# Attention with a gating MLP on one core: where the MLP's seven products are summed, when its matmuls are due, and which engine makes the normalisation's small operations

## The chip, the cores and the metric

One core of one Trainium2 chip. The metric is the time of one execution on the device in microseconds (us), lower is better. The kernel before takes 3404.55 us, the median of three runs (3404.28 to 3408.29).

## What is computed

```python
def _A_ref(x, wqkv, wo):                      # H = 32 heads of 32
    q, k, v = ...                             # x @ wqkv, split by head
    scores = einsum("bhqd,bhkd->bhqk", q, k) * Dh ** -0.5
    p = softmax(scores, axis=-1)
    o = einsum("bhqk,bhkd->bhqd", p, v)
    return o.reshape(B, S, D) @ wo
def _B_ref(x, w1, b1, w2):                    # F = 3584
    h = einsum("bsd,df->bsf", x, w1) + b1
    return einsum("bsf,fd->bsd", mish(h), w2)
xn = layernorm(x)
out = x + _A_ref(xn, wqkv, wo) * silu(_B_ref(xn, w1, b1, w2))
```

Here x is 2048 x 1024, wqkv 1024 x 3072, wo 1024 x 1024, w1 1024 x 3584 and w2 3584 x 1024, all in 32-bit floats.

## The kernel before

Every 32-bit operand of the large matmuls is split into a high part (a copy in the type fp32r, `copy`, ACT, L276) and the rest (`low`, a subtraction, DVE or GpSimd, L284), and each product is made as three matmuls, `THREE`: high x high, high x rest, rest x high. The 2048 rows are 16 tiles of 128 (`NT`), or four chunks of 512 (`NC`). The normalised and transposed x of chunk c stands in `xc0` to `xc3`.

**Stage 1, normalisation and the first pass of v** (to about 85 us). Tile after tile: `x_load` (an issue on SP, the SyncE queue), `ln_a` (statistics on DVE, L398 to L400), `ln_r` (ln and exp on ACT, for the inverse root), `ln_b` (four DVE operations on 128 x 1: one Newton step on the root `rs`, and the shift `tmp`), `ln_x` (the scaling on ACT, L273), `ln_t` (eight transposes on PE, L426), `ln_c` (the split of the transposed tile into `xc`, ACT and DVE). One loop with index t from 2 to 17 runs these for neighbouring tiles, and in between `v_group` (PE, L325) multiplies the tiles that are there with the first 256 columns of v. Instructions of an engine run in the order in which this loop writes them. Beside it, GpSimd splits the first `W1_0` tiles of w1 (`w1_first`): loaded into the two buffers `first_w1`, split into halves of `xc2` and `xc3` that no x tile has reached yet, and moved from there to the DRAM scratch `w1s` (512 KB read and as much written). Each tile of w1 passes through steps 0 (load), 1 (split) and 2 (move) in the iterations n + 2, n + 3 and n + 5:

```python
for step, n in enumerate((t - 2, t - 3, t - 5)):
    if 0 <= n < W1_0:
        w1_first(n, step)
```

Later tiles of w1, up to number 21, are split by GpSimd in the following passes over v.

**Stage 2, q and k** (to about 552 us): the projections `qk`, with splits of w1 and w2 on GpSimd beside them.

**Stage 3, attention and MLP** (to about 3220 us). A planner (`Plan`) merges five streams of operations into one order for each engine. Every operation has an estimated duration, needs, buffers that it takes and gives, and a key, its due time; a simulated clock picks what comes next by these. Attention: scores twice, once for the maximum (`s`, PE; `mx`, DVE) and once transposed (`t`, PE; exponential `p`, ACT); `z`, the sums of the exponentials over tiles, 128 x 2048 additions on GpSimd (L919, 4.6 us each); `pv` (PE). The MLP runs between: `h` (PE), mish (ACT and DVE, some on GpSimd), and `y`. For two of the 28 tiles of F at a time (a pair, `U` = 14 in each chunk) a Strassen scheme makes seven products of 256 x 512, which DVE adds onto seven accumulators, `yacc` (L1213). The due time of a y matmul is set by two numbers, in units of the time of an h tile (g runs from 0 to about 8 within a pair):

```python
g = (2 * j + s + (i + 1) / 3) * 4 / 7
due = 2 * B + 2 + Y0 + g * Y1 + (BEHIND if B >= NC * U - 2 else 0)
```

At the end of each chunk `y_sums` adds the seven products up to the four blocks of y: seven GpSimd additions of 128 x 1024 (L1226), with four stores to the scratch `ys` (SP), each after the sums that it needs. The accumulators are free for the next chunk when those that read them are through.

**Stage 4, the tail** (to the end). The output projection (`op`, L1317) of chunk 0 runs at the end of the plan (`p_stream`), as do the splits of wo. Behind the plan, for chunks 1 to 3: the attention's output is loaded (`oraw`, SP), split (`split_o`: ACT, then DVE, into `ohl` or `xo`), and multiplied tile by tile. For each tile `start` loads x (`x3`) and the finished y (`y3`), ACT makes the silu, and `end` multiplies and adds on DVE (L1420, L1421) and stores to out (issued on ACT's queue, L1425). `x3` and `y3` have six buffers each.

## Time and profile before

| | |
|---|---|
| median of three runs | 3404.55 us |
| the profiled execution | 3404.78 us |
| its span in the trace | 3403.0 us |
| PE (matmul) busy | 3350.0 us, 98% |
| PE weight loads | 2444.7 us, 72% |
| DVE (VectorE) | 2683.6 us, 79% |
| ACT (ScalarE) | 2039.2 us, 60% |
| POOL (GpSimd) | 2727.3 us, 80% |
| read from and written to HBM | 474.97 MB and 160.69 MB |

The span runs from the first instruction to the last; the 1.8 us between it and the execution's time lie around the program. Busy shares are means over four stages with different limits, so what a change in one stage is worth has to be read from that stage. Weight loads run beside matmuls. The profile names tiles without their numbers, and L stands for a line of the listing above.

### The profile page before, as it was taken

The numbers are of one execution on the slowest core, as the hardware profiler recorded it, in microseconds if no ns is written. First come the engines' busy times: TensorE is split into PE (matmuls) and PEld (weight loads), VectorE is DVE, ScalarE is ACT, GpSimd is POOL, SyncE is SP. The second block draws the span as 40 slices with busy tenths as digits, with TensorE's granted clock in tenths as the row PEclk, the third lists the DMA queues.
The fourth block names the chain that finished last, engine by engine and source line by source line (L and its number), as shares of the span: only waits on it lengthen the run. The fifth ranks groups of instructions, "written<-read, shape, count | busy, mean of one in ns | idle before, by whom it ended". The sixth has DMA issues, their size and how long they took to land.

```text
span 3403.0 us, 48050 instructions
## 1 busy us (share of the span) xinstructions
PE 3350.0 (98%) x17107; PEld 2444.7 (72%) x17107; DVE 2683.6 (79%) x4462; ACT 2039.2 (60%) x3394; POOL 2727.3 (80%) x923
## 2 busy tenths in 40 slices
PE   8999999999999999999999999999999999999999
PEld 8898887767766766667777676666776666677587
DVE  6024446999999998889999988889999889896753
ACT  6112222766766667767776677667776776677621
POOL 3547662998898989999989899989988999899910
PEclk9999999999999999999999999999999999999999
DMA  8989997544555465545455564445556555546582
GB/s 285 339 307 370 369 367 243 143 137 138 154 150 148 144 192 180 149 131 153 141 157 157 182 186 137 140 141 148 149 164 198 163 149 158 150 146 193 171 306 85
DMA packets 257633, 639.87 MB, mean 188 GB/s; under 512 B 90266, under 2 KB 99482, under 8 KB 248730
## 3 DMA queue, kind: packets, MB, share of 16 engines
q1 hardware_dynamic: 254948, 628.42, 58.7%
q10 hardware_dynamic: 2448, 8.39, 0.6%
q8 instruction: 136, 2.23, 0.3%
q14 instruction: 101, 0.83, 0.1%
HBM read 474.97 MB, written 160.69 MB: 187 GB/s over the span
## 4 chain that ended last, share of the span: by engine, by line
PE 84%; DVE 7%; DMA 3%; POOL 2%; issue 2%; ACT 1%; SPq 1%; ACTq 0%; DVEq 0%; POOLq 0%
PE h L1049 16%; PE y L1190 13%; PE pv L938 13%; PE s L803 12%; PE t L890 12%; PE qk L725 8%; PE op L1317 4%; PE v L325 4%; DVE mx L809 2%; DMA kstack<-ks 1%; POOL z L919 1%; DVE yacc L1213 1%; ACT p L273 1%; PE zp L974 1%; POOL pw L284 1%
## 5 line engine op out<-in xcount | busy, mean ns | idle before, releaser
L919 POOL TENSOR_TENSOR z<-z,p 128x2048 f32<-128x2048 f32 x448 | 2066.5, 4613 | 75.0 <-ACT p L273 50.6
L273 ACT ACTIVATE p<-t,zero 128x512 f32<-128x512 f32 x2048 | 1366.5, 689 | 455.8 <-PE t L890 436.0
L809 DVE TENSOR_REDUCE mx<-s 128x1 f32<-128x512 f32 x1984 | 1283.4, 682 | 65.9 <-PE s L803 63.4
L890 PE MATMUL t<-qstack,kstack 128*128 128x512 f32 x2048 | 791.3, 394 | 1.8 <-ACT p L273 0.9
L803 PE MATMUL s<-kstack,qstack 128*128 128x512 f32 x1984 | 755.6, 397 | 14.8 <-DMA kstack<-ks 7.5
L1049 PE MATMUL h<-xr,w 128*128 128x512 f32 x2016 | 676.6, 390 | 1.4 <-DVE aw L284 0.6
L1213 DVE TENSOR_TENSOR yacc<-yacc,y 128x512 f32<-128x512 f32 x728 | 492.6, 680 | 36.8 <-PE y L1190 33.3
L803 PEld LDWEIGHTS s<-kstack,qstack 128*128 128x128 f32 x1984 | 366.8, 188 | 160.8 <-issue 26.8
L890 PEld LDWEIGHTS t<-qstack,kstack 128*128 128x128 f32 x2048 | 382.0, 188 | 126.5 <-issue 28.5
L938 PE MATMUL pv<-p,v 128*32 128x512 f32 x4096 | 466.0, 595 | 1.0 <-ACT p L273 0.6
L1049 PEld LDWEIGHTS h<-xr,w 128*128 128x128 f32 x2016 | 377.6, 188 | 84.1 <-DVE aw L284 2.1
L725 PE MATMUL qk<-xc,qkw 128*128 128x512 f32 x1536 | 351.3, 389 | 0.3
L725 PEld LDWEIGHTS qk<-xc,qkw 128*128 128x128 f32 x1536 | 288.0, 188 | 60.8 <-DVE mx L607 1.2
L938 PEld LDWEIGHTS pv<-p,v 128*32 128x32 f32 x4096 | 119.9, 109 | 276.4 <-issue 247.6
L919 POOL TENSOR_TENSOR z<-p,p 128x2048 f32<-128x2048 f32 x32 | 147.8, 4620 | 159.5 <-PE zp L974 107.1
L1190 PE MATMUL y<-w,az 128*128 128x512 f32 x672 | 232.1, 395 | 4.7 <-POOL az L284 1.7
L1190 PE MATMUL y<-w,ay 128*128 128x512 f32 x672 | 227.2, 391 | 3.4 <-ACT ay L276 1.4
L1190 PE MATMUL y<-w,ax 128*128 128x512 f32 x672 | 225.1, 391 | 2.2 <-DVE ax L284 0.7
L1049 PE MATMUL h<-xc,w 128*128 128x512 f32 x672 | 225.7, 391 | 0.0
L950 DVE TENSOR_TENSOR o<-o,pv 128x512 f32<-128x512 f32 x96 | 65.9, 687 | 117.0 <-PE pv L938 112.9
L1190 PEld LDWEIGHTS y<-w,az 128*128 128x128 f32 x672 | 125.1, 189 | 37.1 <-DVE yacc L1213 3.1
L1190 PEld LDWEIGHTS y<-w,ay 128*128 128x128 f32 x672 | 125.2, 188 | 33.2 <-DVE yacc L1213 3.5
(134 smaller groups left out, 3627.8 us busy)
## 6 DMA issues: line engine op xcount, KB each, us to landing
w<-w2s SPq DMA_DIRECT2D x392, 512.0 KB
w<-w1s SPq DMA_DIRECT2D x224, 512.0 KB
w2s<-pw SPq DMA_DIRECT2D x98, 512.0 KB
qstack<-qs SPq DMA_DIRECT2D x96, 256.0 KB
kstack<-ks SPq DMA_DIRECT2D x96, 256.0 KB
w1s<-w1h SPq DMA_DIRECT2D x34, 512.0 KB
x<-in_A_x_dram SPq DMA_DIRECT2D x32, 512.0 KB
qs<-qst SPq DMA_DIRECT2D x32, 512.0 KB
```

The costliest lines, as they stand in the source:

```text
L273: nc.scalar.activation(out_, in_, fn, bias=zero if bias is None else bias, scale=scale)
L325: nc.tensor.matmul(ps[:, :cols], xc[t // 4][:, a, k, (t % 4) * P:(t % 4 + 1) * P], w(b, k), start=n == 0, stop=n == 3 * KT - 1)
L725: nc.tensor.matmul(ps, w[:, k // 4, a, k % 4], xc[c][:, b, k], start=n == 0, stop=n == 3 * KT - 1)
L803: nc.tensor.matmul(sp_, qst[h % 3][:, qt * P:(qt + 1) * P], kst[h % 3][:, kc * 512:(kc + 1) * 512], start=True, stop=True)
L809: nc.vector.reduce_max(tiles["mx"][:, qt, kc:kc + 1], tiles[qt, kc], axis=AX.X)
L890: nc.tensor.matmul(tp, kst[h % 3][:, kt * P:(kt + 1) * P], qst[h % 3][:, c * 512:(c + 1) * 512], start=True, stop=True)
L919: nc.gpsimd.tensor_tensor(zs[h], pts[T - 1] if kt == 1 else zs[h], pts[T], ALU.add)
L938: nc.tensor.matmul(t["b"][c * DH:(c + 1) * DH, :], vt[h][:, k, :], pts[T - kt + k][:, c * 512:(c + 1) * 512], start=k == kt - size + 1, st ...
L1049: nc.tensor.matmul(t["h"], w1t[m_][:, a, k % 4], xts_[c][:, b, k], start=i == 0, stop=i == 3 * KT - 1)
L1190: nc.tensor.matmul(t["y"], acts[B, kind][:, p, half * 256 + s * P:half * 256 + (s + 1) * P], w2t[m_][:, q], start=i == 0, stop=i == 2)
L1213: nc.vector.tensor_tensor(ya, ya, t["y"], ALU.subtract)
L1317: nc.tensor.matmul(ps[t, dh], ohl[t // 4, k][:, a, s * P:(s + 1) * P], wt[k][b][:, r], start=k == 0 and i == 0, stop=k == KT - 1 and i == 2)
```

## The change

Five edits. (1) `W1_0` is 3 instead of 4; all three tiles of w1 are staged in `xc3`, each half is split in an iteration of its own (t = 5 to 10), and the moves stand in iterations 7, 9 and 11 (before: 5 to 8). The first x tile is loaded and scaled in two halves. (2) From the third tile on, `ln_b` runs on GpSimd, as six operations with two inputs or one. (3) `Y1` is 0.18 instead of 0.14. (4) For chunks 1 to 3 `y_store` stores the seven products as they are, each after DVE's last addition to it; `ys` holds seven blocks of 256 x 512 for each chunk, 3.67 MB instead of 2.1. Chunk 0 keeps `y_sums`. (5) In the tail the blocks are loaded into `yp` in two calls, one at the first tile of the chunk before and one at its second; at its third tile `y_total` adds them up on GpSimd, and the silu is made in two halves. `x3` has five buffers.

```diff
@@ -24,7 +24,7 @@
-W1_0, W1_V = 4, 21
+W1_0, W1_V = 3, 21
 
 PACE = 1.95
 NS = H * NT
@@ -36,7 +36,7 @@
 
-PS, ACTS, W1S, W2S, Y0, Y1 = 6, 4, 3, 3, 1.2, 0.14
+PS, ACTS, W1S, W2S, Y0, Y1 = 6, 4, 3, 3, 1.2, 0.18
 
@@ -243,7 +243,7 @@
-    ys = [dram.tile([P, 4, D], F32, name=f"ys{i}") for i in range(NC)]
+    ys = [dram.tile([P, 7, 2, 512], F32, name=f"ys{i}") for i in range(NC)]
@@ -359,27 +359,27 @@
 
     def x_load(t):
         xt = vp.tile([P, D], F32, tag="x", name=f"x{t}", bufs=5)
-        nc.sync.dma_start(xt, x[t * P:(t + 1) * P, :])
+        for r in (slice(0, 512), slice(512, D)) if t == 0 else (slice(0, D),):
+            nc.sync.dma_start(xt[:, r], x[t * P:(t + 1) * P, r])
         return xt
 
     first_w1 = [p.tile([P, 2, KT, P], F32, tag=tag, name=f"w1f{tag}") for p, tag in ((w1p, "z0"), (big, "w"))]
 
-    def split_w(w, raw, job=False):
-        for half in range(2):
+    def split_w(w, raw, job=False, halves=range(2)):
+        for half in halves:
             r = slice(half * 4, half * 4 + 4)
             p = w[half] if isinstance(w, list) else w[:, half]
             (nc.gpsimd if job else nc.vector).tensor_copy(p[:, 0], raw[:, r])
             low(nc.gpsimd if job else nc.vector, p[:, 1], raw[:, r], p[:, 0])
 
     def w1_first(n, step):
-        t, g = xc[2 + n // 2], n % 2
-        raw = first_w1[n // 2][:, g]
-        w = t[:, 1, 4 * g:4 * g + 4].rearrange("p k n -> p (k n)") \
+        raw = first_w1[n // 2][:, n % 2]
+        w = xc[NC - 1][:, n // 2, 4 * (n % 2):4 * (n % 2) + 4].rearrange("p k n -> p (k n)") \
             .rearrange("p (h a k f) -> p h a k f", h=2, a=2, f=P)
         if step == 0:
             nc.sync.dma_start(raw, w1[n])
-        elif step == 1:
-            split_w(w, raw, True)
+        elif step < 3:
+            split_w(w, raw, True, (step - 1,))
         else:
             move(w1s[n], w)
 
@@ -408,6 +408,16 @@
     def ln_b(t):
         mv, var, rs = stat.pop(t)
         tmps[t] = tmp = vp.tile([P, 1], F32, tag="tmp", name=f"tmp{t}", bufs=3)
+        if t > 1:
+            g = nc.gpsimd
+            g.tensor_tensor(tmp, rs, var, ALU.mult)
+            g.tensor_tensor(tmp, tmp, rs, ALU.mult)
+            g.tensor_scalar(tmp, tmp, -0.5, 1.5, op0=ALU.mult, op1=ALU.add)
+            g.tensor_tensor(rs, rs, tmp, ALU.mult)
+            g.tensor_tensor(tmp, mv[:, 0:1], rs, ALU.mult)
+            g.tensor_scalar(tmp, tmp, -1.0, 0.0, op0=ALU.mult, op1=ALU.add)
+            tmps[t] = tmp, rs
+            return
         nc.vector.scalar_tensor_tensor(tmp, rs, var, rs, op0=ALU.mult, op1=ALU.mult)
         nc.vector.tensor_scalar(tmp, tmp, -0.5, 1.5, op0=ALU.mult, op1=ALU.add)
         nc.vector.tensor_tensor(rs, rs, tmp, ALU.mult)
@@ -416,7 +426,8 @@
 
     def ln_x(t):
         tmp, rs = tmps.pop(t)
-        act(xts[t], xts[t], AF.Identity, bias=tmp, scale=rs)
+        for r in (slice(0, 512), slice(512, D)) if t == 0 else (slice(0, D),):
+            act(xts[t][:, r], xts[t][:, r], AF.Identity, bias=tmp, scale=rs)
 
     def ln_t(t):
         xt = xts.pop(t)
@@ -475,8 +486,11 @@
         if t + 1 < NT:
             ln_r(t + 1)
         evac()
-        for step, n in enumerate((t - 2, t - 3, t - 5)):
-            if 0 <= n < W1_0:
+        if t - 2 < W1_0:
+            w1_first(t - 2, 0)
+        for step in (3, 1, 2):
+            n, odd = divmod(t - 4 - step, 2)
+            if not odd and 0 <= n < W1_0:
                 w1_first(n, step)
         if t == NT - 3:
             vraw = {(i, 0): v_load(1 + i, 0) for i in range(2)}
@@ -1214,7 +1228,7 @@
                     done[j, s] = op("DVE" if b else "ACT", 0.69 if b else 0.6, emit=y_add, urgent=U_Y,
                                     give=[("d", t["own"]), ("b", t["own"])], need=[m] + ([free[j]] if j in free and b == 0 else []))
             if b == U - 1:
-                free = y_sums(c, done)
+                free = (y_store if c else y_sums)(c, done)
         final["y"] = m
 
     def y_sums(c, done):
@@ -1227,23 +1241,30 @@
             last[i] = free[i] = free[j] = o
             return o
 
-        def store(j, rh, dh):
+        def store(j):
             def emit(at):
-                nc.sync.dma_start(ys[c][:, 2 * rh:2 * rh + 2, dh * 512:(dh + 1) * 512], yacc[:, j])
+                nc.sync.dma_start(ys[c][:, j], yacc[:, j])
             free[j] = op("SP", 0.1, need=[last[j]], emit=emit, bytes_=P * 1024 * 4)
 
         add_(4, 0)
         add_(0, 2)
-        store(0, 0, 0)
+        store(0)
         add_(1, 4)
         add_(3, 1)
-        store(3, 1, 0)
+        store(3)
         add_(4, 5)
         add_(4, 6)
-        store(4, 0, 1)
+        store(4)
         add_(5, 1)
-        store(5, 1, 1)
+        store(5)
         return free
+
+    def y_store(c, done):
+        def store(j):
+            return op("SP", 0.1, need=[done[j, i] for i in range(2)], bytes_=P * 1024 * 4,
+                      emit=lambda at: nc.sync.dma_start(ys[c][:, j], yacc[:, j]))
+
+        return {j: store(j) for j in range(7)}
 
@@ -1389,7 +1410,8 @@
     ph = ExitStack()
     op_ = pool(ph, "op", 8)
     rp = pool(ph, "rp", 8, side="right")
-    xp = pool(ph, "xp", 6, side="right")
+    xp = pool(ph, "xp", 5, side="right")
+    yp = pool(ph, "yp", 2, side="right")
     oraw = {}
 
     def new_o(c, k):
@@ -1408,17 +1430,33 @@
         low(nc.vector, o[:, 1], raw, o[:, 0])
 
     xt, yt = {}, {}
+    BLOCK = {(0, 0): 0, (1, 0): 3, (0, 1): 4, (1, 1): 5}
 
     def start(t):
         xt[t] = xp.tile([P, D], F32, tag="x3", name=f"x3_{t}")
         nc.sync.dma_start(xt[t], x[t * P:(t + 1) * P, :])
-        yt[t] = xp.tile([P, D], F32, tag="y3", name=f"y3_{t}")
-        nc.sync.dma_start(yt[t], ys[t // 4][:, t % 4])
+
+    def y_load(c, js):
+        for j in js:
+            yt[c, j] = yp.tile([P, 2, 512], F32, tag=f"y{j}", name=f"yp{c}_{j}", bufs=2 if j in BLOCK.values() else 1)
+            nc.sync.dma_start(yt[c, j], ys[c][:, j])
+
+    def y_total(c):
+        for i, j in ((4, 0), (0, 2), (1, 4), (4, 5), (4, 6), (3, 1), (5, 1)):
+            nc.gpsimd.tensor_tensor(yt[c, i], yt[c, i], yt[c, j], ALU.add)
+
+    def silu(t):
+        c, s = divmod(t, 4)
+        for dh in range(2):
+            y = yt[c, BLOCK[s // 2, dh]][:, s % 2]
+            act(y, y, AF.Silu)
 
     def end(t, dh):
+        c, s = divmod(t, 4)
+        y = yt[c, BLOCK[s // 2, dh]][:, s % 2]
         r = slice(dh * 512, dh * 512 + 512)
-        nc.vector.tensor_tensor(yt[t][:, r], ps[t, dh], yt[t][:, r], ALU.mult)
-        nc.vector.tensor_tensor(xt[t][:, r], xt[t][:, r], yt[t][:, r], ALU.add)
+        nc.vector.tensor_tensor(y, ps[t, dh], y, ALU.mult)
+        nc.vector.tensor_tensor(xt[t][:, r], xt[t][:, r], y, ALU.add)
         if t == NT - 1:
             nc.scalar.dma_start(out[t * P:, r], xt[t][:, r])
         elif dh:
@@ -1426,9 +1464,13 @@
 
     for k in range(KT):
         new_o(1, k)
-    for t in range(4):
-        start(t)
-    act(yt[0], yt[0], AF.Silu)
+    start(0)
+    y_load(0, (0, 4))
+    start(1)
+    y_load(0, (3, 5))
+    start(2)
+    start(3)
+    silu(0)
     for k in range(4):
         split_o(1, k)
     for c in range(NC):
@@ -1436,12 +1478,16 @@
             t = 4 * c + s
             if t + 4 < NT:
                 start(t + 4)
+            if c + 1 < NC and s < 2:
+                y_load(c + 1, ((4, 0, 2, 1), (5, 6, 3))[s])
+            if c + 1 < NC and s == 2:
+                y_total(c + 1)
             for dh in range(2):
                 k = 2 * s + dh
                 if c + 1 < NC and (c or k > 3):
                     split_o(c + 1, k)
                 if dh == 0 and t + 1 < NT:
-                    act(yt[t + 1], yt[t + 1], AF.Silu)
+                    silu(t + 1)
                 if c:
                     n = 2 * s + dh
                     ps[t, dh] = bank({"b": bank_of[n]}, f"op{t}_{dh}")
```

What this does to the engines' order is shown at three places, by the lines of each kernel's own listing (the changed kernel's are 14 higher in the plan and 23 to 38 higher in the tail).

**The normalisation, around tile 6.** First DVE's instructions before the change: `st`, `mv` and `var` are the statistics of tile 7, `rs6` and `tmp6` root and shift of tile 6, and the last two rows are the split of tile 5's transposes (`pt5`).

```order
L398 BN_STATS st7_504<-x7_372 128x6 x2
L399 BN_AGGR mv7_505<-st7_504 128x2
L400 TENSOR_SCALAR var7_506<-mv7_505 128x1
L411 SCALAR_TENSOR_TENSOR tmp6_523<-rs6_442,var6_441 128x1
L412 TENSOR_SCALAR tmp6_523<-tmp6_523 128x1
L413 TENSOR_TENSOR rs6_442<-rs6_442,tmp6_523 128x1
L414 SCALAR_TENSOR_TENSOR tmp6_523<-mv6_440,rs6_442 128x1
L284 TENSOR_TENSOR xc1_173<-pt5_0_537,xc1_173 128x4x128
L284 TENSOR_TENSOR xc1_173<-pt5_1_542,xc1_173 128x4x128
```

GpSimd's instructions there after the change; `w1fz0` is a loaded tile of w1, and the rows on `xc3` are the two operations of a half of its split.

```order
L372 CAST xc3_175<-w1fz0_179 128x512
L284 TENSOR_TENSOR xc3_175<-w1fz0_179,xc3_175 128x512
L413 TENSOR_TENSOR tmp6_521<-rs6_446,var6_445 128x1
L414 TENSOR_TENSOR tmp6_521<-tmp6_521,rs6_446 128x1
L415 TENSOR_SCALAR tmp6_521<-tmp6_521 128x1
L416 TENSOR_TENSOR rs6_446<-rs6_446,tmp6_521 128x1
L417 TENSOR_TENSOR tmp6_521<-mv6_444,rs6_446 128x1
L418 TENSOR_SCALAR tmp6_521<-tmp6_521 128x1
L372 CAST xc3_175<-w1fz0_179 128x512
```

The four operations on `rs6` and `tmp6` have left DVE, which goes from the statistics straight to the split of `pt5`; on GpSimd six stand in their place, between one half of a w1 tile and the next.

**GpSimd at the end of chunk 2.** Before the change; `z24` collects the exponentials of a head from the tiles `p`, `g84` and `az42` belong to the activation.

```order
L919 TENSOR_TENSOR z24_25684<-z24_25684,p398_26300 128x2048
L1226 TENSOR_TENSOR yacc_5157<-yacc_5157 128x1024
L1131 TENSOR_TENSOR g84_26232<-g84_26232 128x256
L1226 TENSOR_TENSOR yacc_5157<-yacc_5157 128x1024
L284 TENSOR_TENSOR az42_26459<-g84_26232,az42_26459 128x512
L1226 TENSOR_TENSOR yacc_5157<-yacc_5157 128x1024 x5
L284 TENSOR_TENSOR hl0_2352<-nm26_0_26540,hl0_2352 128x16
L919 TENSOR_TENSOR z24_25684<-z24_25684,p399_26355 128x2048
```

After it, at the same place:

```order
L933 TENSOR_TENSOR z24_25708<-z24_25708,p398_26321 128x2048
L933 TENSOR_TENSOR z24_25708<-z24_25708,p399_26357 128x2048
L1145 TENSOR_TENSOR g84_26330<-g84_26330 128x256
L284 TENSOR_TENSOR az42_26517<-g84_26330,az42_26517 128x512
L933 TENSOR_TENSOR z25_26561<-p400_26407,p401_26471 128x2048
```

The seven additions on `yacc` are gone, and the z additions follow each other, with only the activation's two operations between them.

**The tail, ACT's and SP's queues while chunk 0 ends.** ACT before the change; `oraw1_5` to `oraw1_7` are the attention's outputs of chunk 1, and `y3_4` is the finished y of tile 4.

```order
L276 ACTIVATE ohl1_5_32537<-oraw1_5_32538 128x512
L1425 DMA out_0_dram<-x3_2_32554 128x1024
L276 ACTIVATE ohl1_6_32540<-oraw1_6_32541 128x512
L273 ACTIVATE y3_4_32573<-y3_4_32573,zero_143 128x1024
L276 ACTIVATE ohl1_7_32543<-oraw1_7_32544 128x512
```

ACT after it; `yp1_0` and `yp1_4` are two of the seven blocks of chunk 1.

```order
L276 ACTIVATE ohl1_5_32562<-oraw1_5_32563 128x512
L1463 DMA out_0_dram<-x3_2_32583 128x1024
L276 ACTIVATE ohl1_6_32565<-oraw1_6_32566 128x512
L273 ACTIVATE yp1_0_32601<-yp1_0_32601,zero_143 128x512
L273 ACTIVATE yp1_4_32599<-yp1_4_32599,zero_143 128x512
L276 ACTIVATE ohl1_7_32568<-oraw1_7_32569 128x512
```

And the loads on SP's queue behind those of the tail's start, after the change:

```order
L1437 DMA x3_4_32597<-in_A_x_dram 128x1024
L1442 DMA yp1_4_32599<-ys1_136 128x1024
L1442 DMA yp1_0_32601<-ys1_136 128x1024
L1442 DMA yp1_2_32603<-ys1_136 128x1024
L1442 DMA yp1_1_32605<-ys1_136 128x1024
L1437 DMA x3_5_32614<-in_A_x_dram 128x1024
L1442 DMA yp1_5_32616<-ys1_136 128x1024
L1442 DMA yp1_6_32618<-ys1_136 128x1024
L1442 DMA yp1_3_32620<-ys1_136 128x1024
```

On ACT the silu is in the same place, in halves, but it reads blocks that GpSimd has to sum first. On SP the seven loads of chunk 1 stand around x tile 5, which takes the buffer of x tile 0 and so waits for the store of tile 0; before, one `y3` load followed each `x3` load.

## The prediction

> **What bounds the kernel now.** I read the windows of the stages first, then in each stage the groups by line, the waits and the timeline.
>
> ```profile
> 15.00:44.00 29.00, 27.50 (x225) 26.81 (x224) 26.84 (x72) 21.66 (x44) 15.12 (x17) 1.00 0.88 300
> 44.00:59.00 15.00, 15.00 (x131) 14.99 (x130) 13.03 (x40) 12.28 (x25) 0.00 (x0) 1.00 1.03 402
> 59.00:74.00 15.00, 12.81 (x97) 12.61 (x96) 9.00 (x26) 9.56 (x19) 0.00 (x0) 0.89 0.67 229
> 85.00:552.00 467.00, 465.84 (x2230) 392.08 (x2229) 171.93 (x224) 91.97 (x174) 290.10 (x238) 1.00 0.93 343
> 552.00:3100.00 2548.00, 2523.26 (x12993) 1763.89 (x12993) 2288.04 (x3846) 1767.70 (x2924) 2271.37 (x617) 1.00 0.53 156
> 3100.00:3235.00 135.00, 126.87 (x643) 86.92 (x642) 97.89 (x136) 90.72 (x150) 131.30 (x38) 0.99 0.59 185
> 3235.00:3403.00 168.00, 162.77 (x715) 133.55 (x713) 66.64 (x92) 32.10 (x41) 6.75 (x3) 1.00 0.53 194
> ```
>
> The columns are the stretch, its length, then busy time of PE, weight loads, DVE, ACT and POOL, the granted clock, the DMA share and GB/s. PE is the bound almost everywhere: it idles 1.2 us in 85 to 552, 24.7 in 552 to 3100, 8.1 in 3100 to 3235 and 5.2 behind that. Time can come only from this idle time, or from the first 85 us, where PE's own busy time is no floor yet. There, the normalisation, PE's work is short and DVE is nearly as busy (26.84 of 29).
>
> ```profile
> 15.02 1.58 PE L426 MATMUL pt<-ident,x 128*128 128x128 f32 x8
> 43.76 1.03 PE L426 MATMUL pt<-ident,x 128*128 128x128 f32 x8
> 58.78 1.03 PE L426 MATMUL pt<-ident,x 128*128 128x128 f32 x8
> 73.94 1.04 PE L426 MATMUL pt<-ident,x 128*128 128x128 f32 x8
> ...
> 50.45 10.55 DMA x<-in_A_x_dram
> ...
> PE v L325 <- DVE xc L284: 3.6, 3, 2.2
> ```
>
> These are the transposes of tiles 1, 8, 12 and 15. Tiles 8 to 12 come at (58.78-43.76)/4 = 3.755 us each, with PE without a gap: that is PE's pace. Tiles 1 to 8 take 28.74/7 = 4.11 us each, and 12 to 15 take 15.16 us for three, since the x tile issued at 50.45 lands only 10.55 us later, behind transfers that fill the engines (1.03 at 402 GB/s). So 28.74 - 7 x 3.755 = 2.4 and 15.16 - 3 x 3.755 = 3.9 us are lost there, 6.3 together.
>
> **The change part by part.** *The normalisation's small operations.* In the first stretch below (10 to 43 us, GpSimd at work on w1) and in the second (43 to 60, GpSimd idle) DVE's four cost:
>
> ```profile
> L411 DVE SCALAR_TENSOR_TENSOR tmp<-rs,var 128x1 f32<-128x1 f32 x8 | 2.7, 337 | 1.4 <-ACT rs L273 1.4
> L413 DVE TENSOR_TENSOR rs<-rs,tmp 128x1 f32<-128x1 f32 x8 | 2.6, 330 | 0.3
> L414 DVE SCALAR_TENSOR_TENSOR tmp<-mv,rs 128x1 f32<-128x1 f32 x8 | 1.6, 197 | 0.3
> L412 DVE TENSOR_SCALAR tmp<-tmp 128x1 f32<-128x1 f32 x8 | 1.2, 154 | 0.3
> ...
> L411 DVE SCALAR_TENSOR_TENSOR tmp<-rs,var 128x1 f32<-128x1 f32 x4 | 0.8, 210 | 0.0
> L413 DVE TENSOR_TENSOR rs<-rs,tmp 128x1 f32<-128x1 f32 x4 | 0.6, 160 | 0.1
> ```
>
> 337 + 330 + 197 + 154 = 1.02 us a tile leave DVE; at 26.84 of 29 us busy that takes it well under PE's pace, so tiles 1 to 8 fall to 3.755 if GpSimd keeps up. No row shows a 128x1 operation of GpSimd with two inputs; the nearest is its 128x16:
>
> ```profile
> L284 POOL TENSOR_TENSOR hl<-nm,hl 128x16 fp32r<-128x16 f32 x31 | 7.0, 227 | 7.6 <-ACT hl L276 7.5
> 25.16 0.63 POOL L371 CAST xc<-w1fz 128x512 fp32r<-128x512 f32 x1 [9.98 <-DMA w1fz<-in_B_w_dram]
> 25.88 1.30 POOL L284 TENSOR_TENSOR xc<-w1fz,xc 128x512 fp32r<-128x512 f32 x1
> L273 ACT ACTIVATE x<-x,tmp,rs 128x1024 f32<-128x1024 f32 x15 | 18.6, 1243 | 9.1 <-DVE tmp L414 8.2 <-POOL xc L371 1.0
> L273 ACT ACTIVATE rs<-rs,zero 128x1 f32<-128x1 f32 x14 | 4.1, 294 | 0.5
> L273 ACT ACTIVATE rs<-var,zero 128x1 f32<-128x1 f32 x14 | 3.9, 281 | 2.4 <-DVE var L400 2.4
> ```
>
> A dependent operation follows 0.09 us behind (25.16 + 0.63 to 25.88), so six take 6 x (0.227 + 0.09) = 1.9 us. The new ring is: GpSimd's six, ACT's x (1.24), ACT's two rs (0.28 + 0.29) and two hand-overs, say 0.1: 1.9 + 1.24 + 0.57 + 0.1 = 3.8 us, just PE's pace. Bounds for one operation: 0.15 us (DVE's cheapest) to 1.3 (GpSimd's 128x512); I take the 128x16 row. In the six iterations where half a w1 tile (0.63 + 0.09 + 1.30 = 2.0) stands between two chains, GpSimd needs 3.9 a tile; I charge 0.5 us. GpSimd's w1 work no longer stretches DVE's small operations, as there are none left behind tile 1.
>
> [...]
>
> *The w1 tiles split early.* Three instead of four, with their 1 MB moves two iterations apart: ahead of the x tile that lands late stand 2 MB of moves and 0.5 MB of loads less, 6.2 us at 402 GB/s. Its 10.55 us shrink to about 4.4, and the 3.9 us go, as the tile is then there when DVE asks for it. The fourth w1 tile is loaded and split behind 85 us, beside PE-bound work (1.2 us of idle in 467); if that cover failed, its 1.5 MB would cost 4 us. What is late next: the third move now leaves `xc3` only at iteration 11, and tile 12 is written there one and a half iterations on; 1 MB at 402 GB/s plus what is queued can hold DVE's copy. I charge 1.0 us (0 to 3).
>
> *The first tile in halves.* Half of ACT's 1.24 us no longer stands before the first transposes, 0.6 us less; the x1 load behind it is issued one instruction later. I take 0.5 (0 to 1.2). The stage gives 6.3 + 0.5 - 1.0 - 0.5 = **5.3 us**, and all of it moves the PE-bound work behind it forward.
>
> *The seven products of chunks 1 to 3.*
>
> ```profile
> 1966.00:1986.00 20.00, 19.46 (x82) 14.49 (x81) 19.29 (x35) 16.25 (x30) 19.84 (x10) 1.00 0.89 271
> 2640.00:2656.00 16.00, 13.51 (x52) 9.03 (x51) 15.38 (x28) 8.96 (x17) 15.92 (x9) 1.00 0.82 248
> ...
> 2634.65 2.40 POOL L1226 TENSOR_TENSOR yacc<-yacc 128x1024 f32<-128x1024 f32 x1
> ...
> 2641.88 11.91 POOL L1226 TENSOR_TENSOR yacc<-yacc 128x1024 f32<-128x1024 f32 x5
> ...
> PE s L803 <- DMA kstack<-ks: 7.5, 7, 2.0
> PE s L803 <- DVE mx L809: 3.3, 7, 1.0
> PE y L1190 <- DVE yacc L1213: 3.0, 7, 0.6
> ```
>
> Seven sums hold GpSimd's z chain for 17 us, the exponentials get no p tile, and PE runs out of t. During the sums of chunk 1 PE idles 20 - 19.46 = 0.54 us, of chunk 2 16 - 13.51 = 2.49. The change takes these away: **3.0 us** (bounds 0, if DVE at 15.38 of 16 is the limit there, and 5). Chunk 0 keeps its sums. Each later chunk stores 1.5 MB more beside a DMA share of 0.53, which hides it.
>
> *Wider due times.* A chunk pair's y matmuls spread over 0.18/0.14 = 1.29 times as long. The waits they take part in are those above, 13.8 us in all. The spread takes peaks off DVE (the yacc and mx waits, 6.3 us, a quarter of which is 1.5) but holds activations and banks longer. Bounds 5 less and 5 more; I take **1.5 us** less.
>
> *The tail.*
>
> ```profile
> 3217.98 20.97 POOL L1226 TENSOR_TENSOR yacc<-yacc 128x1024 f32<-128x1024 f32 x7
> ...
> 3239.43 4.68 SPq L1403 DMA_DIRECT2D oraw<-ot  x8
> ...
> 3272.07 0.70 DVE ohl L284
> 3272.77 0.04 issue
> 3272.81 125.67 PE op L1317 x553
> ...
> L284 DVE TENSOR_TENSOR xo<-or,xo 128x512 fp32r<-128x512 f32 x8 | 20.0, 2547 | 0.0
> ...
> L284 DVE TENSOR_TENSOR ohl<-oraw,ohl 128x512 fp32r<-128x512 f32 x16 | 10.8, 688 | 20.0 <-ACT ohl L276 20.0
> ```
>
> PE is dense here; its one stall ends at 3272.81, on the split of `ohl` 7 of chunk 1. Today SP stands on ys stores until GpSimd's sums end at 3238.95 and issues the tail's loads right behind; the new stores wait for DVE alone, so loads can start up to 9 us sooner; the first still waits for memory that DVE and GpSimd use, so I take 5. Against it: ACT now runs the silu of tile 4 before the copy for `ohl` 7, as before, but that silu needs five of GpSimd's seven sums of chunk 1, and their last blocks are loaded behind x tile 5, which waits for the first store of out. By then 8 x 0.25 + 6 x 0.5 + 2 + 3.5 + 0.5 = 11 MB have moved: at the stage's busy 342 GB/s (DMA share 0.97 from 3239 to 3260)
>
> ```profile
> 3239.00:3260.00 21.00, 21.00 (x94) 17.41 (x93) 7.66 (x10) 5.56 (x7) 2.75 (x1) 1.00 0.97 342
> ```
>
> 32 us from 3234.4, so 3266.6; two sums of 2.40, silu, copy and split (0.6 to 0.7 each) give 3273.3 for the split's end, against 3272.77. I charge **0.5 us** (from 0.7 less to 9 more: no earlier start, 5, and the adds and DVE's two-input operations in each other's way, 2 x (2.55 - 0.69) = 3.7).
>
> [...]
>
> *Sum.* 5.3 + 3.0 + 1.5 - 0.5 = 9.3 us less than the profiled execution's 3404.78 (span 3403.0), 3395.5; the median of the runs is 0.2 below that execution, so **3395**.
>
> **The rivals.** *The sums were hidden anyway* (and the wider times give back what they take): PE has other work during most of a burst, and idle there is short. Only the first stage and the tail move: 3404.8 - 5.3 + 0.5 = 3400. For it: DVE near 1.0 in both windows.
> *The tail's sums come late*: +9 instead of +0.5, 3404. For it: DVE's 2547 ns beside GpSimd; against it, the sooner start of SP.
> [...]
> [...]
>
> **How the numbers follow.** Forecast 0.55, hidden sums 0.20, late tail 0.09, slow six 0.09, slower 0.07. A measurement of this kernel can tell about 0.2%, 6.8 us, from no change, so faster means below 3397.7: 0.50 of the forecast's share, 0.05 of the hidden sums', 0.03 of the others: 0.58. Slower means above 3411: the 0.07, and 0.03 where a late tail meets a poor first stage. The rest, 0.32, is the same. Low end: 7.5 + 5 + 5 + 0.7 = 18 less, 3386. High end: the late tail with a weak attention, 3406; beyond both lie about 2 in 10.
>
> **What would show it.** Right: transposes of tile 15 near 68 to 69 us; GpSimd's 128x1 operations near 0.23; no x load over 6 us; no idle PE near the ends of chunks 1 and 2; the tail's first loads 4 to 9 us closer behind the last attention matmul; the stall before chunk 1 of at most 2 us. Wrong: ACT's x waiting for GpSimd in each iteration, DVE waiting for the w1 move at tile 12, PE waiting 5 us or more for `ohl` 7, or more PE idle in 552 to 3100 than 24.7 us, which would lay it to the due times.

## The result, and the profile after

The changed kernel takes **3386.31 us**, the median of five runs (3385.42 to 3388.82), against 3404.57 of the kernel before: 0.9946 of it, with a 95% interval of 0.9935 to 0.9957. That is 18.3 us less where 9.3 were forecast; the time lies at the very low end of the range. The profiled execution took 3385.42 us. Below are the row of the busy times from its page, and the windows of the stages, with the columns of the prediction's first fence.

```profile
PE 3340.2 (99%) x17107; PEld 2446.9 (72%) x17107; DVE 2691.8 (80%) x4406; ACT 2041.7 (60%) x3411; POOL 2747.1 (81%) x1007
```

```profile
85.00:552.00 467.00, 465.80 (x2230) 392.05 (x2229) 171.83 (x227) 92.32 (x175) 294.19 (x243) 1.00 0.94 347
552.00:3100.00 2548.00, 2532.21 (x13092) 1778.91 (x13091) 2302.49 (x3868) 1785.82 (x2954) 2262.18 (x609) 1.00 0.54 159
3100.00:3235.00 135.00, 129.43 (x640) 91.50 (x639) 88.28 (x130) 80.61 (x132) 94.55 (x28) 0.99 0.73 247
3235.00:3383.00 148.00, 140.04 (x606) 114.52 (x604) 80.46 (x75) 26.55 (x44) 56.29 (x21) 0.97 0.52 184
```

PE makes the same 17107 matmuls. In 552 to 3100 us it now idles 15.8 us instead of 24.7, and it starts 13092 matmuls there instead of 12993: more work in the same time. From 3235 to the end it idles 8.0 us instead of 5.2, at a mean clock of 0.97 instead of 1.00.

Fixed windows can't say how far the one kernel is ahead of the other. So I followed PE's matmuls in the order of their starts, counted each by its pitch, the time from start to start when matmuls stand back to back (0.227 us for 128x512, 0.112 for `pv`), and compared the times at which two kernels had done the same amount. The first column is the kernel before; the others are the leads (minus) or lags against it, each from one profiled execution. The names behind `after` are experiments, told below.

```
before at us           after  y1_alone sums_alone norm_alone y1_back
 574.9 (plan starts)   -2.8    -1.6     -2.1       -2.2       -3.2
1242.5                 -7.8    -5.5     -1.7       -2.9       -4.2
1400.6 (chunk 0 ends)  -2.8    -1.7     -0.4       -1.9       -3.6
1964.5                 -4.3    -4.2     +0.7       -2.6       -3.0
2176.1 (chunk 1 ends) -12.1    -5.6     -8.2       -2.3      -12.0
2586.0                -14.8    -8.0     -9.2       -3.0      -13.0
2794.6 (chunk 2 ends) -18.9   -11.0    -13.8       -3.6      -17.3
3050.9                -21.7   -10.3    -14.5       -3.9      -18.0
3265.0 (tail starts)  -24.8   -12.3    -15.8       -4.1      -19.5
3366.4                -19.5    -5.5     -8.3       -4.4       -9.6
```

The last row agrees within 0.2 us with the differences of the spans (19.4, 5.5, 8.1, 4.3 and 9.5). In `after`, 2.8 us come from ahead of the plan and 5.0 from chunk 0, whose end takes 5.0 back; 7.8 come around the end of chunk 1, 4.1 around that of chunk 2, 5.9 behind that, and 5.3 are lost in the tail.

### The profile page after: what moved, and what is told of

Its sections match the earlier page's. It is cut to its first block, busy times and chain, and to the rows that moved or that the text cites. A ratio compares the mean times of both kernels' runs of the same rounds, so it can differ in the third digit from the quotient of the medians.

```text
span 3383.6 us, 48201 instructions
## 1 busy us (share of the span) xinstructions
PE 3340.2 (99%) x17107; PEld 2446.9 (72%) x17107; DVE 2691.8 (80%) x4406; ACT 2041.7 (60%) x3411; POOL 2747.1 (81%) x1007
## 5 line engine op out<-in xcount | busy, mean ns | idle before, releaser
L817 PE MATMUL s<-kstack,qstack 128*128 128x512 f32 x1984 | 764.5, 396 | 8.5 <-DMA kstack<-ks 5.7
L1063 PE MATMUL h<-xr,w 128*128 128x512 f32 x2016 | 692.7, 391 | 0.7 <-ACT p L273 0.4
L817 PEld LDWEIGHTS s<-kstack,qstack 128*128 128x128 f32 x1984 | 367.7, 188 | 150.3 <-issue 24.7
L1204 PE MATMUL y<-w,ay 128*128 128x512 f32 x672 | 238.0, 393 | 6.0 <-DMA w<-w2s 2.9
L1063 PE MATMUL h<-xc,w 128*128 128x512 f32 x672 | 232.6, 390 | 0.0
```

The source lines that it names most:

```text
L817: nc.tensor.matmul(sp_, qst[h % 3][:, qt * P:(qt + 1) * P], kst[h % 3][:, kc * 512:(kc + 1) * 512], start=True, stop=True)
L1063: nc.tensor.matmul(t["h"], w1t[m_][:, a, k % 4], xts_[c][:, b, k], start=i == 0, stop=i == 3 * KT - 1)
L1204: nc.tensor.matmul(t["y"], acts[B, kind][:, p, half * 256 + s * P:half * 256 + (s + 1) * P], w2t[m_][:, q], start=i == 0, stop=i == 2)
```

## The experiments

All were timed over five rounds beside runs of the kernel before (medians 3404.8 to 3405.1). The first four take the change apart. My theory by then was that the attention's gain comes from GpSimd's sums; the rivals were the due times, and an order of the plan so sensitive that parts don't add.

**Due times alone** (`y1_alone`), on the kernel before:

```diff
-PS, ACTS, W1S, W2S, Y0, Y1 = 6, 4, 3, 3, 1.2, 0.14
+PS, ACTS, W1S, W2S, Y0, Y1 = 6, 4, 3, 3, 1.2, 0.18
```

> The kernel before with the due times of y widened alone (0.14 to 0.18). Where one follows the same amount of PE work through both traces, the changed kernel gains 5.1 us between 552 and 1250 us, where only the due times differ, loses 5.6 around the end of chunk 0, and gains some 22 behind it, up to the tail. Due times as the source of the attention's gain: at least 12 us less than before, about 3390. Sums as the source: chunk 0's minus 5 and plus 5 are all that this kernel shows, 3404, within 3. The plan's order is chaotic, so that any edit moves it by several us and parts do not add: any value between 3390 and 3415.

3399.37 us, 0.9984 (0.9975 to 0.9993) of before: 5.5 less, between the two theories, and so inside the wide band of the third. The gain in chunk 0 (3.9 us) and a loss at its end (3.8) are there.

**Stored products and tail alone** (`sums_alone`), edits 4 and 5 on the kernel before:

```diff
-                free = y_sums(c, done)
+                free = (y_store if c else y_sums)(c, done)
...
```

> The kernel before with the seven stored products of chunks 1 to 3 and the sums in the tail alone (edits 4 and 5); normalisation and due times as before. Sums as the source of the attention's gain: 17 to 22 us less in the attention, 5 more in the tail (PE waits there 4 us for the last split of chunk 1, behind a silu that waits for the sums, and runs at a lower clock behind it), so 3404.6 - 15 = 3390. Due times as the source: 3 less at most in the attention (the PE idle in the bursts, forecast 3.0) and 5 more in the tail, so 3404 to 3408.

3396.17 us, 0.9972 (0.9961 to 0.9984): 8.7 less, again between the two. The attention gains 13.7, and the tail loses 7.5 instead of 5.

**Normalisation alone** (`norm_alone`), edits 1 and 2 on the kernel before:

```diff
-W1_0, W1_V = 4, 21
+W1_0, W1_V = 3, 21
...
+            g = nc.gpsimd
+            g.tensor_tensor(tmp, rs, var, ALU.mult)
...
```

> The kernel before with edits 1 and 2 alone (three early tiles of w1, first tile in halves, small operations on GpSimd). The first stage of the changed kernel is 2.8 us shorter and the plan behind it is the same as before: if stages add, 3401.8, within 1. If the plan's stage takes up or gives back part of an earlier start: 3400 or less, or 3404.

3407.45 us, 1.0002 (0.9994 to 1.0011): no gain, and above every band of the expectation; the profiled execution was the fastest of eleven (3400.76). This is the forecast's largest term.

**The changed kernel with the old due times** (`y1_back`):

```diff
-PS, ACTS, W1S, W2S, Y0, Y1 = 6, 4, 3, 3, 1.2, 0.18
+PS, ACTS, W1S, W2S, Y0, Y1 = 6, 4, 3, 3, 1.2, 0.14
```

> The changed kernel with the due times back at 0.14. Due times as the source: it loses nearly all of the attention's gain, 3400 to 3405. Sums as the source: 3386 to 3390. If parts add, this is 3404.6 plus what sums_alone and norm_alone change, to 1 us, and the changed kernel's 3386.3 minus this is what y1_alone changes; if they do not add by over 3 us, the two edits of the plan work on one another.

3395.68 us, 0.9972 (0.9961 to 0.9984), in neither band. It is where `sums_alone` is, so edits 1 and 2 add nothing here either. From here to the changed kernel the due times bring 9.4 us, more than the 5.5 alone, though the intervals are too wide to be sure of that difference.

The next four ask for mechanisms. **GpSimd's bursts put back, without their purpose** (`burst_back`), on the changed kernel:

```diff
+        done_ = {}
+
+        def burst(i, j):
+            need = [done_.get(x) or done[x, s] for x in (i, j) for s in range(2)]
+            done_[i] = op("POOL", 2.4, need=need, key=-1,
+                          emit=lambda at: [nc.gpsimd.tensor_tensor(spare, spare, spare, ALU.add) for _ in range(6)])
+        if c < NC - 1:
+            for i, j in ((4, 0), (0, 2), (1, 4), (3, 1), (4, 5), (4, 6), (5, 1)):
+                burst(i, j)
         return {j: store(j) for j in range(7)}
...
     yacc = mlp.tile([P, 7, 2, 512], F32, name="yacc")
+    spare = mlp.tile([P, 128], F32, name="spare")
+    nc.gpsimd.memset(spare, 0.0)
```

> The changed kernel with GpSimd's bursts put back at the ends of chunks 1 and 2, without their purpose: where the sums stood, seven operations of GpSimd, each six additions of 128x128 on a spare tile, with the needs and the price that the sums had in the plan; the stores and the accumulators wait for none of them. It computes the same. GpSimd's time as the cost of the sums: 3386 + 12 (7.5 at the end of chunk 1, 4.5 at the end of chunk 2, as the kernel with the sums removed alone had them) = 3398, with PE idle over 3 us in 1950 to 2190 again. The accumulators that are held until the sums are through as the cost: 3386 to 3389, and PE idle below 1 us there.

3402.26 us, 0.9992 (0.9984 to 1.0001): 16 us back, where 12 were expected; six of these additions took 2.81 us where a sum takes 2.40. The windows around the end of chunk 1 show where it goes. The kernel before:

```profile
1950.00:2190.00 240.00, 235.59 (x1207) 161.09 (x1209) 210.03 (x352) 167.69 (x280) 218.04 (x62) 1.00 0.53 156
```

`sums_alone`:

```profile
1950.00:2190.00 240.00, 239.83 (x1252) 168.28 (x1251) 214.63 (x361) 172.78 (x291) 214.46 (x59) 1.00 0.55 165
```

`burst_back`:

```profile
1950.00:2190.00 240.00, 232.21 (x1192) 161.56 (x1185) 205.73 (x345) 166.16 (x279) 219.81 (x97) 0.99 0.53 161
```

PE idles 4.41 us with the sums, 0.17 without them, 7.79 with the empty bursts. Nothing waits for the empty bursts' results, so GpSimd's time alone is enough to cost what the sums cost. The two fall in different places, though. The empty burst ends at 1990.7, and PE's longest wait is right there, for the z addition behind it:

```profile
1995.39 1.93 PE L988 MATMUL zp<-z,ones 128*32 128x512 f32 x8 [5.08 <-POOL z L933]
```

Against the changed kernel all of its loss around chunk 1 (9.6 us, followed as in the table of leads) comes from 1980 to 2010. In the kernel before, the burst ends at 1983, only 0.54 us of the idle time lie in it, and 3.87 lie behind 2020; against `sums_alone` it loses 1.0 us from 1965 to 1980, nothing more up to 2070, and 8.0 from there to 2175, where PE's visible waits are mostly for loads of `kstack`. PE, DVE and ACT are seen waiting for no sum from 1950 to 2190 there, but SP's queue, in which loads stand behind the stores, waits 6.2 us for them; the empty burst leaves that wait out. Whether the late loss comes from it, or from another order in the plan, stays open.

**Another order of the silu on ACT, and two early tiles of w1** (`tail_two`), on the changed kernel:

```diff
-W1_0, W1_V = 3, 21
+W1_0, W1_V = 2, 21
...
-                if dh == 0 and t + 1 < NT:
+                if dh == (s == 3) and t + 1 < NT:
                     silu(t + 1)
```

> The changed kernel with the silu of the next chunk's first tile behind the last split of that chunk in ACT's queue, and with two early tiles of w1 instead of three. If the tail's 5.3 us are the split that stands behind a silu that waits for GpSimd's sums: PE's wait of 4.0 us before chunk 1's matmuls and the lower clock behind it go, 5 us less, unless the banks that the end of tile 4 frees come late next (then 2 less at most). If the third move of w1 is what holds the split of tile 12 in the first stage: no wait of DVE there, tile 13's transposes 3.74 us behind tile 12's instead of 5.62, 1.9 less. Together 3379; if neither, 3386.

3384.15 us, 0.9940 (0.9927 to 0.9952). The early tiles of w1 came out as expected (below); the tail did not get better. In the changed kernel the timelines of ACT, DVE and PE have these rows around the end of chunk 0:

```profile
3248.46 0.72 ACT L273 ACTIVATE yp<-yp,zero 128x512 f32<-128x512 f32 x1 [3.39 <-POOL yp L1446]
3249.09 0.61 ACT L276 ACTIVATE ohl<-oraw 128x512 fp32r<-128x512 f32 x1
...
3237.71 2.88 DVE L284 TENSOR_TENSOR ohl<-oraw,ohl 128x512 fp32r<-128x512 f32 x1
...
3240.52 0.68 DVE L1458 TENSOR_TENSOR yp<-op,yp 128x512 f32<-128x512 f32 x1
3241.23 2.18 DVE L1459 TENSOR_TENSOR x<-x,yp 128x512 f32<-128x512 f32 x1
...
3249.73 2.00 DVE L284 TENSOR_TENSOR ohl<-oraw,ohl 128x512 fp32r<-128x512 f32 x1 [0.76 <-ACT ohl L276]
...
3249.75 1.22 PE L1338 MATMUL op<-wo,ohl 128*128 128x512 f32 x2 [2.99 <-ACT ohl L276]
3251.79 10.47 PE L1338 MATMUL op<-wo,ohl 128*128 128x512 f32 x38 [0.81 <-DVE ohl L284]
```

And in `tail_two`:

```profile
3245.34 0.34 ACTq L1463 DMA_DIRECT2D out_dram<-x  x1
...
3250.77 2.82 DVE L284 TENSOR_TENSOR ohl<-oraw,ohl 128x512 fp32r<-128x512 f32 x1
...
3253.65 8.52 PE L1338 MATMUL op<-wo,ohl 128*128 128x512 f32 x25 [4.48 <-DVE ohl L284]
```

With the silu out of the way, ACT's copies stand behind the issue of a store that waits for DVE, and the split of `ohl` 7 ends at 3253.6 instead of 3251.7. DVE's splits and additions take 1.7 to 2.9 us each while GpSimd sums, and 0.69 before and after. In the changed kernel ACT's copy of `ohl` 7, behind the silu that waits 3.39 us for GpSimd, ends PE's wait of 2.99; with that silu moved, the split on DVE ends a wait of 4.48. So ACT's order alone is not the bound.

**Due times wider still** (`y1_wider`), on the changed kernel:

```diff
-PS, ACTS, W1S, W2S, Y0, Y1 = 6, 4, 3, 3, 1.2, 0.18
+PS, ACTS, W1S, W2S, Y0, Y1 = 6, 4, 3, 3, 1.2, 0.24
```

> The changed kernel with the due times wider still, 0.24 instead of 0.18. If a wider spread by itself saves PE the short waits (below 0.8 us each, 14.8 us in 600 to 1250 at 0.14 and 9.7 at 0.18), the same stretch has 6 or less, and the end of chunk 0, where the spread cost 3 us of idle PE, costs more: 3380 to 3388. If 0.18 is a lucky order among many: any value from 3384 to 3400, and the short waits of that stretch are above 9.7.

3419.21 us, 1.0046 (1.0032 to 1.0060), outside all that was expected. Followed as in the table of leads, the loss against the changed kernel grows through the whole plan, from 2.5 us at 575 to 32 at 3265, and PE's idle time doesn't show it. The same window in the kernel before, in `y1_alone` and in `y1_wider`:

```profile
600.00:1250.00 650.00, 647.52 (x3353) 451.79 (x3351) 605.12 (x1021) 454.39 (x757) 578.51 (x154) 1.00 0.52 148
```

```profile
600.00:1250.00 650.00, 647.94 (x3384) 453.56 (x3383) 608.64 (x1028) 460.41 (x762) 585.77 (x158) 1.00 0.52 150
```

```profile
600.00:1250.00 650.00, 647.81 (x3340) 449.01 (x3338) 603.67 (x1017) 459.03 (x758) 579.21 (x156) 1.00 0.51 146
```

PE's busy time is the same within 0.5 us, but the work is not: `y1_alone` starts 32 matmuls of `pv` more than the kernel before and as many others (3.6 us of work by the pitches), `y1_wider` as many of `pv` and 13 others fewer (2.9 us). A matmul of 128x512 is shown with 0.39 us and the next can start 0.227 us later, so a gap of up to 0.16 us between two leaves no idle time. Taken from start to start of neighbouring 128x512 matmuls, the gaps above 0.227 us come to 12.8, 9.9 and 16.3 us in these windows, where the busy time shows 2.5, 2.1 and 2.2 idle. That is the sign of the expectation's second reading, an order that happens to suit.

**The small operations on DVE again** (`dve_small`), on the changed kernel:

```diff
-        if t > 1:
+        if t >= NT:
             g = nc.gpsimd
```

> The changed kernel with the normalisation's small operations on DVE again, as four. If GpSimd's six are what brings tiles 1 to 8 to PE's pace of 3.74 us: tile 8's transposes 0.7 to 1.7 us later than with them (43.7 instead of 42.1 to 43.0). As the third move of w1 holds tile 12 until about 62 us in either case, the stage then ends where it did, and the time stays at 3386; if nothing else holds tile 12, 1 to 2 us more.

3389.10 us, 0.9955 (0.9942 to 0.9967), 2.8 more; its interval and the changed kernel's overlap, so a cost in time is not shown. Tile 8 came at 43.72 us, as expected.

Three more ask what would be better. **All splits of chunk 1 ahead of the tail's loop, two early tiles of w1** (`splits_first`), on the changed kernel:

```diff
-W1_0, W1_V = 3, 21
+W1_0, W1_V = 2, 21
...
-    for k in range(4):
+    for k in range(KT):
         split_o(1, k)
...
-                if c + 1 < NC and (c or k > 3):
+                if c + 1 < NC and c:
```

> The changed kernel with all eight splits of chunk 1 ahead of the tail's loop instead of four, so that none of them runs while GpSimd sums, and with two early tiles of w1 (as in tail_two, whose silu stays where the changed kernel has it). If the tail's loss is DVE's slowness beside GpSimd (its x additions took 2.13 to 2.18 us there and the splits 1.7 to 2.9, against 0.69 apart from GpSimd's work), which the last four splits of chunk 1 stood behind: PE goes from chunk 0 to chunk 1 without a wait, and 5.3 us go with the lower clock; 2 more with the third w1 move, 3379. If the banks come late instead (the ends of tiles 0 to 3, behind four more splits on DVE): PE waits for DVE's products in place of the splits, and 3384 as tail_two.

**3375.69 us**, 0.9916 (0.9902 to 0.9929): 29 us less than before and 10.6 less than the changed kernel. The same window of the changed kernel and of this one:

```profile
3235.00:3260.00 25.00, 21.05 (x82) 16.26 (x81) 20.69 (x16) 5.87 (x10) 18.62 (x7) 0.86 0.83 291
```

```profile
3235.00:3260.00 25.00, 25.00 (x112) 20.71 (x111) 17.27 (x15) 5.17 (x8) 16.80 (x7) 1.00 0.86 301
```

PE starts 112 matmuls instead of 82, without idle time and at the full clock, with GpSimd's sums still in the middle of it.

**Due times between** (`y1_less`), on the changed kernel:

```diff
-PS, ACTS, W1S, W2S, Y0, Y1 = 6, 4, 3, 3, 1.2, 0.18
+PS, ACTS, W1S, W2S, Y0, Y1 = 6, 4, 3, 3, 1.2, 0.16
```

> The changed kernel with due times of 0.16. 0.14 gave 3395.7, 0.18 gives 3386.3 and 0.24 gave 3419.2. A trend with an optimum near 0.18: 3389 to 3393. One order among many, each some us off another without a trend: anything from 3384 to 3410, and outside 3389 to 3393.

3390.53 us, 0.9956 (0.9942 to 0.9969), inside the band of a trend: 3395.7, 3390.5 and 3386.3 at 0.14, 0.16 and 0.18, and 3419.2 at 0.24. These runs spread over 9 us, though.

**Without chunk 0's sums** (`no_sums_0`), on the changed kernel:

```diff
-                free = (y_store if c else y_sums)(c, done)
+                free = y_store(c, done)
```

> The changed kernel that leaves out chunk 0's seven sums: its seven products are stored as the other chunks', the tail loads four of them as they are, so the first 512 rows lack their sums. It says what the one burst that is left costs at these due times. By the kernels with and without bursts, one costs 5 to 8 us: 3379 to 3381, the gain between 1280 and 1450 us. If the wide due times are themselves what costs idle PE at the end of chunk 0 (4.9 us in 1290 to 1420 against 1.5 to 2.3 at 0.14): 3384 to 3387.

3379.19 us, 0.9926 (0.9914 to 0.9938), 7.1 less. The windows of the changed kernel and of this one:

```profile
1290.00:1420.00 130.00, 125.07 (x634) 85.84 (x630) 108.97 (x182) 88.52 (x148) 115.29 (x36) 1.00 0.56 171
```

```profile
1290.00:1420.00 130.00, 129.90 (x685) 90.80 (x678) 111.54 (x188) 97.37 (x165) 115.03 (x33) 1.00 0.60 179
```

PE idles 0.10 us instead of 4.93. So it is the sums that cost there, more so with the wide due times (1.72 us idle in the kernel before). How much of that is GpSimd's time this run doesn't say: in the changed kernel ACT waits 2.1 us there for an accumulator that is being stored.

**Chunk 0's sums between additions of z** (`spread_0`), on `splits_first`:

```diff
-            o = op("POOL", 2.4, need=need, key=-1,
+            o = op("POOL", 2.4, need=need,
```

> The kernel of splits_first with the sums of chunk 0 queued on GpSimd by the time at which each is ready instead of ahead of all else, so that additions of z come between them (two, two and three sums, with a z addition behind each group). It computes the same. If it is the length of the burst that starves the exponentials of buffers and PE of work, most of the 5 to 10 us of the end of chunk 0 go: 3368 to 3372. If GpSimd's time counts wherever it stands: 3374 to 3377. If the accumulators, held longer, stop the next chunk's products: above 3377.

3378.76 us, 0.9922 (0.9908 to 0.9935), against 0.9916 of `splits_first`: nothing gained. By its band that is the third case, the accumulators that are held, but PE's only wait in 1290 to 1420 that touches them is 0.6 us behind one of ACT's copies. Contrary to the expectation it doesn't compute the same: the sum that reads accumulator 4 and the next that writes it can change places, so the first 512 rows are mixed from other products, with as many sums of the same size. GpSimd's timeline:

```profile
1301.47 4.88 POOL L1240 TENSOR_TENSOR yacc<-yacc 128x1024 f32<-128x1024 f32 x2
1306.30 4.63 POOL L933 TENSOR_TENSOR z<-z,p 128x2048 f32<-128x2048 f32 x1
1310.90 4.87 POOL L1240 TENSOR_TENSOR yacc<-yacc 128x1024 f32<-128x1024 f32 x2
...
1320.43 7.03 POOL L1240 TENSOR_TENSOR yacc<-yacc 128x1024 f32<-128x1024 f32 x3
```

The order is as meant, with a z addition behind each group, and PE idles 4.6 us in 1290 to 1420 (125.36 busy of 130), as much as with the burst in one piece (4.5). So GpSimd's 17 us seem to count whether in one piece or three.

## Why the prediction came out as it did

The direction was right and the range just held the time, but the gain is twice the forecast. Of its four terms the largest gain (5.3) came to nothing, the other two gains (3.0 and 1.5) were far too small and lie beyond their own bounds (5 each), and so was the loss in the tail (0.5). That the range held the time is luck: the misses cancel. The rival in which the sums were hidden fell; the one in which the tail's sums come late is what happened in the tail, beside gains that outweigh it.

The premise under all of it, "Time can come only from this idle time", is what failed first. From start to start of neighbouring 128x512 matmuls, the gaps above the pitch of 0.227 us come to 67 us in 552 to 3100 in the kernel before and to 51 in the changed one; idle time shows 23 and 15 us of these.

**The normalisation, forecast 5.3 less: about nothing.** The part on the ring was right. GpSimd's six run as forecast or faster:

```profile
L413 POOL TENSOR_TENSOR tmp<-rs,var 128x1 f32<-128x1 f32 x8 | 1.5, 189 | 8.4 <-ACT rs L273 8.4
```

189 ns instead of 227, 0.27 us from start to start, and tiles 3 to 12 go at 3.74 us, PE's pace. Two of the chances, 0.09 and 0.07, are for slower operations, whose times no run shows: 189 ns lies between DVE's 160 (L413) and 210 (L411) in 43 to 60 us of the kernel before. The step that failed is the late x tile, 3.9 us: I took it from one execution. The first stage is the same program in the kernel before, `y1_alone` and `sums_alone`. All the profiled executions, by the times of the transposes (`tile 8`, the steps between tiles 12, 13 and 14) and by the first matmul of the next pass:

```
kernel         w1 tiles  tile 8   12-13  13-14  next pass
before             4      43.76    6.82   4.60    79.6
y1_alone           4      43.65    5.18   3.73    77.0
sums_alone         4      43.73    5.07   3.74    76.9
after              3      43.00    5.62   3.74    76.7
norm_alone         3      42.79    6.11   3.74    77.0
y1_back            3      42.05    5.73   3.75    75.9
burst_back         3      43.14    6.87   4.59    79.0
y1_wider           3      43.34    6.41   4.78    78.9
y1_less            3      43.19    7.95   5.69    81.2
no_sums_0          3      42.68    5.63   3.74    76.4
dve_small          3      43.72    6.92   4.91    79.9
tail_two           2      42.71    3.74   3.74    74.6
splits_first       2      43.00    3.74   3.74    74.8
spread_0           2      42.72    3.74   3.74    74.6
```

The quoted execution had a late tile of 3.1 us and 0.9 behind it at a lower clock; the other two of the same program lose 1.3 to 1.4. And the third move, priced at 1.0 us (0 to 3), costs 1.9 to 4.2 between tiles 12 and 13. It is the one that was named: in the changed kernel DVE's timeline has

```profile
62.01 1.29 DVE L284 TENSOR_TENSOR xc<-pt,xc 128x512 fp32r<-128x512 f32 x2 [3.28 <-DMA w1s<-xc]
```

and with two early tiles the wait is gone in three kernels of three. The mean end of the stage is 77.8 with the old code and 77.9 in the seven with three tiles and GpSimd's operations; 74.7 with two. The edit was right but for its third tile. The halves of the first tile, too, seem to give back what they gain: in the eleven kernels with halves the first transposes come 0.1 to 0.8 us sooner (8.18 to 8.86, for 8.95 to 8.99), those of tile 2 mostly later (18.87 to 20.73, for 18.82 to 19.19). What holds tile 2 was not tested.

**The sums, forecast 3.0 less: about 12 to 14 in the attention.** That a burst on GpSimd costs PE time was right, the size was not. The step that failed is "During the sums ... PE idles": I counted idle time in windows of 20 and 16 us around the bursts, but in the kernel before PE loses most of it later, 90 to 190 us behind the burst's end, and half of it in gaps too short to show as idle time. What the sums of chunk 1 cost is the step of 8 to 9 us between 1964 and 2176 in the table of leads, in all three kernels without them, against +0.3 and -1.4 in the two that keep them; chunk 2 adds 4.1 to 4.6, though `y1_alone`, which keeps its sums, gains 3.0 there too. The bound of 5 was as short as the windows. The path that the forecast gave (no p tile, PE out of t) is not the one seen: with the empty burst PE waits for z, in the kernel before for `kstack`.

**The due times, forecast 1.5 less: 5.5 alone (interval 2.4 to 8.5) and 9.4 without the sums.** The bound of 13.8 us of waits was a bound on visible idle time only; what the wider spread saves in chunk 0 are mostly gaps too short to be seen, as the three windows of 600 to 1250 show. Why a spread of 0.24 loses them again stays open, and so whether 0.18 is the best.

**The tail, forecast 0.5 more (at most 9): 5.3 more, and 7.5 and 9.9 in the two kernels without wide due times.** PE did wait for `ohl` 7 of chunk 1: the split ended at 3251.7, and PE had run out of other work at 3246.8, so the place was right. The term that was mis-sized is the one of DVE and GpSimd in each other's way, taken for two operations of 3.7 us in all and kept for the upper end. Six stood in that stretch: three splits (2.88, 1.72, 2.00) and three additions (2.17, 2.18, 2.13), 13.1 us instead of 6 x 0.69 = 4.1. `tail_two` shows that the order of ACT alone was not the cause, and `splits_first`, which moves four splits ahead of the sums, that the splits beside the sums were. (`y1_alone`, whose sums stand where they stood before, loses 6.8 in another way. SP issues its tail's loads only behind the last sums, at 3231.25, 8.2 us sooner than in the kernel before, where PE is 12 us ahead; that this is the cause was not tested.) Not every operation of DVE was slower, as its rows above show: the multiplication, which reads one input from PSUM (L1458), takes 0.68 us in the midst of the sums, as it does behind them at 3256.27, and the addition behind it (L1459), with two inputs in SBUF, takes 2.18 there and 0.69 at 3256.99. What holds the addition was not shown.

The terms as measured, 0, -12 to -14, -5.5 to -9.4 and +5.3, give 12 to 18 less, against 18.3: it takes the upper ends. Sums and due times may help one another, but the intervals of these runs do not show it.

## What to carry to other kernels

The burst on GpSimd, which feeds a long chain, was not priced by PE's idle time inside it (0.54 us in chunk 1's, where 8 to 9 were lost by 2176): look for it until the chain has caught up, or put the burst back empty and see. Idle time of PE is a lower bound where a matmul's record is longer than its pitch (0.39 us against 0.227 here); compare the work done by a given time. And one profiled execution of a stage that waits for DMA is one draw (the step from tile 12 to 13 took 6.82, 5.18 and 5.07 us in three of one program): where a term rests on a late transfer, see it in a second execution, or give it the range of the shortest such transfers.

## What the runs showed of the hardware

PE's clock after a wait was the surprise. In the first stage, where PE waits around tile 12 for the split of `xc`, the kernel before and `norm_alone` have these rows:

```profile
64.15 1.65 PE L325 MATMUL v<-vw,xc 128*128 128x256 f32 x6 [2.19 <-DVE xc L284]
```

```profile
63.04 0.98 PE L325 MATMUL v<-vw,xc 128*128 128x256 f32 x6 [2.12 <-DVE xc L284]
```

The waits are nearly the same, but the six matmuls behind them take 1.65 us in the first and 0.98 in the second. The granted clock from 64 to 66 us is 0.50 in the first and 1.00 in the second, and the step from tile 13 to 14 is 4.60 and 3.74 us. Other waits here that were followed by 0.50 lasted from 1.84 us (`y1_wider`) to 3.32 (`y1_less`). So the length of a wait did not decide alone here. In the tail of the changed kernel, with matmuls counted behind the busy time:

```profile
3246.00:3250.00 4.00, 0.86 (x3) 0.44 (x3) 3.21 (x4) 1.24 (x2) 4.00 (x2) 0.79 0.45 150
3250.00:3254.00 4.00, 3.19 (x7) 2.10 (x8) 3.97 (x3) 0.00 (x0) 3.95 (x2) 0.50 0.98 292
3254.00:3258.00 4.00, 4.00 (x16) 3.21 (x15) 2.81 (x5) 2.38 (x4) 0.00 (x0) 0.86 1.03 383
```

With an idle of 2.99 us the clock is at half for 6.8 us in all, (0.21 + 0.50 + 0.14) x 4 / 0.5, and waits of 3.8 us in all cost 5.3. So waits of 1.84 to 3.32 us were followed by the half clock here, and one of 2.12 was not. What decides between them no run here tested.
